# Block 0 of a two-layer kernel: tiles 2 and 3 turned by DMA, V in two halves, eps added on GpSimd, one input tile loaded later

## The chip, the cores and the metric

The kernel runs on one core of a Trainium2 chip. The metric is the device time of one execution in microseconds (us).

PE is TensorE (matmul), PEld its weight load, DVE is VectorE, ACT is ScalarE, POOL is GpSimd, SP is the engine that issues nearly all DMAs.

## The reference, cut to what matters

```python
x = x + A(layernorm(x), wqkv, wo)     # local attention, 32 heads of 32, window 8, dilation 2
x = x + B(layernorm(x), W_gate, W_up, W_down)   # (relu(gate) * up) @ W_down
x = x + A(...); x = x + B(...)        # once more, same weights
# x: 2048 x 1024 bf16
```

The kernel works in four blocks of 512 tokens, each of four tiles of 128 tokens. The layer norm makes `xn` (tokens on partitions); the projections need it turned, `xnT` (features on partitions). V, Q and K of block 0 are the first real work of TensorE.

## The kernel before

The norm of block 0, where the program starts. All four tiles are turned by TensorE (`turn`: eight 128x128 transposes into PSUM, then two copies); tiles 2 and 3 in between the V chunks.

```python
def aggr(t):                                   # DVE: mean, var, then var + eps
    ...
    on("v", nc.vector.tensor_scalar, vpe[t][:], mv[:, 1:2], EPS, None, op0=ALU.add)
    power(t)
def power(t):                                  # POOL: (var + eps) ** -0.5
    on("g", nc.gpsimd.tensor_tensor, rstd[t][:], vpe[t][:], neg_half[:, 0:1], op=ALU.pow)
...
hold["later"] = {2: (lambda: (turn(2), copy(2, "a", 0), copy(2, "v", 1))),
                 4: (lambda: (turn(3), copy(3, "v", 0), copy(3, "a", 1)))}

def v_first(ln):                               # (chunk, first tile, last tile + 1)
    plan = [(c, 0, 2) for c in range(6)] + [(c, 2, 4) for c in range(6)] + [(c, 0, 4) for c in range(6, KC)]
...
QK_FIRST = [(nm, c) for c in range(KC) for nm in ("q", "k")]          # block 0: q0 k0 q1 k1 ...
```

After Q and K of block 0, VectorE makes the q-k products of that block, then its softmax and its sum over V, then the products of block 1: one chain. Every 512-wide result of TensorE goes into one of six PSUM banks and holds it until ScalarE or VectorE has read it.

Of the kernel before, what the change touches and what calls it, by code (L numbers as in the profile page):

```python
# [9 lines left out]
ALU = mybir.AluOpType  # L10
ACT = mybir.ActivationFunctionType
# [3 lines left out]
D = 1024  # L15
# [5 lines left out]
KC = D // P  # L21
BLK = 512
TPB = BLK // P
# [13 lines left out]
def kernel(  # L37
# [130 lines left out]
        xt = xpool.tile([P, D], BF16, name=f"x{t}")  # L168
        x_tiles.append(xt)

    def load_x(b):
        for t in range(b * TPB, (b + 1) * TPB):
            if t == 0:
                sp_dma(x_tiles[t][:, 0:SLAB], x_dram[t * P:(t + 1) * P, 0:SLAB])
                nc.scalar.dma_start(x_tiles[t][:, SLAB:D], x_dram[t * P:(t + 1) * P, SLAB:D])
            elif t == 2:
                nc.scalar.dma_start(x_tiles[t][:], x_dram[t * P:(t + 1) * P, :])
            else:
                sp_dma(x_tiles[t][:], x_dram[t * P:(t + 1) * P, :])

    load_x(0)


    slab = {}
# [5 lines left out]
    def want_v(key, mid, end):  # L190
        for g in range(2):
            want((key, g), wqkv_v[:, :, 2 * D + g * SLAB:2 * D + (g + 1) * SLAB], mid if g == 0 else end)
# [105 lines left out]
    def ln_first():  # L298
        hold = {"xnT": xnT_pool.tile([P, TPB, KC, P], BF16, tag="xnT", name="xnT_first")}
        xna = big_tile([P, TPB, D], "xn_first", True)  # L300
        last = {}

        def on(eng, f, *args, **kwargs):
            if eng == "v":
                dv(f, *args, **kwargs)
            elif eng in last:
                with tc.issue_after(last[eng]):
                    last[eng] = f(*args, **kwargs).ins
            else:
                last[eng] = f(*args, **kwargs).ins  # L310

        def small(name, bufs=4):
            return stat_pool.tile([P, 1], F32, tag="f" + name, name=name, bufs=bufs)

        mean, vpe, rstd, bst = {}, {}, {}, {}

        def bn(t, half):
            if half == 0:
                bst[t] = stat_pool.tile([P, 2, 6], F32, tag="bst", name="bst")
            on("v", nc.vector.bn_stats, bst[t][:, half, :], x_tiles[t][:, half * SLAB:(half + 1) * SLAB])  # L320

        def aggr(t):
            mv = stat_pool.tile([P, 2], F32, tag="mv", name="mv", bufs=4)
            on("v", nc.vector.bn_aggr, mv[:], bst[t][:].rearrange("p a b -> p (a b)"))
            vpe[t], mean[t] = small("vpe1"), mv[:, 0:1]
            on("v", nc.vector.tensor_scalar, vpe[t][:], mv[:, 1:2], EPS, None, op0=ALU.add)
            power(t)

        def power(t):
            rstd[t] = small("rstd1")  # L330
            on("g", nc.gpsimd.tensor_tensor, rstd[t][:], vpe[t][:], neg_half[:, 0:1], op=ALU.pow)

        def act_stats(t):
            st1 = stat_pool.tile([P, 2], F32, tag="st1", name="st1")
            on("a", nc.scalar.activation, xna[:, t, :], x_tiles[t][:], ACT.Identity, accum_out=st1[:, 0:1])
            on("a", nc.scalar.activation, xna[:, t, :], x_tiles[t][:], ACT.Square, accum_out=st1[:, 1:2])
            return st1

        def act_vpe(t, st1):
            mn = small("mean1")  # L340
            on("v", nc.vector.tensor_scalar, mn[:], st1[:, 0:1], 1.0 / D, None, op0=ALU.mult)
            nvar = small("nvar1")
            on("v", nc.vector.scalar_tensor_tensor, nvar[:], st1[:, 0:1], mn[:], st1[:, 1:2], op0=ALU.mult, op1=ALU.subtract)
            vpe[t], mean[t] = small("vpe1"), mn[:]
            on("v", nc.vector.tensor_scalar, vpe[t][:], nvar[:], -1.0 / D, EPS, op0=ALU.mult, op1=ALU.add)
            power(t)

        def apply(t):
            on("v", nc.vector.tensor_scalar, xna[:, t, :], x_tiles[t][:], mean[t], rstd[t][:],
               op0=ALU.subtract, op1=ALU.mult)  # L350

        tps = {}

        def turn(t):
            tps[t] = [psum.tile([P, KC // 2, P], BF16, tag="acc", name=f"tp{h}") for h in range(2)]
            for c in range(KC):
                with pe_group():
                    tail_pe[0] = nc.tensor.transpose(tps[t][c // (KC // 2)][:, c % (KC // 2), :],  # L358
                                                     xna[:, t, c * P:(c + 1) * P], ident[:]).ins

        def copy(t, eng, h):
            f = nc.vector.tensor_copy if eng == "v" else nc.scalar.copy
            on(eng, f, hold["xnT"][:, t, h * (KC // 2):(h + 1) * (KC // 2), :], tps[t][h][:])

        warm = small("warm")
        on("a", nc.scalar.activation, warm[:], ones[:, 0:1], ACT.Identity)
        scratch(14)
        bn(0, 0)
        bn(0, 1)
        aggr(0)  # L370
        bn(1, 0)
        bn(1, 1)
        aggr(1)
        st1 = act_stats(2)
        apply(0)
        turn(0)
        apply(1)
        copy(0, "a", 1)
        copy(0, "a", 0)
        turn(1)  # L380
        act_vpe(2, st1)
        copy(1, "v", 0)
        copy(1, "a", 1)
        bn(3, 0)
        bn(3, 1)
        apply(2)
        aggr(3)
        apply(3)
        hold["later"] = {2: (lambda: (turn(2), copy(2, "a", 0), copy(2, "v", 1))),
                         4: (lambda: (turn(3), copy(3, "v", 0), copy(3, "a", 1)))}  # L390
        return hold


# [20 lines left out]

    def v_first(ln):
        st = att[0]
        plan = [(c, 0, 2) for c in range(6)] + [(c, 2, 4) for c in range(6)] + [(c, 0, 4) for c in range(6, KC)]

        def f_(i, c, t0, t1):
            def f():  # L420
                if i == 0:
                    st["vT"] = big_tile([P, KC, BLK], "vT_0", True)
                acc = psum.tile([P, BLK], F32, tag="acc", name="acc_v")
                cols = slice(t0 * P, t1 * P)
                with pe_group():
                    for kc in range(KC):
                        mm(acc[:, cols], lhsT=slab[("v0", c // 4)][:, kc, (c % 4) * P:(c % 4 + 1) * P],
                           rhs=ln["xnT"][:, t0:t1, kc, :], start=(kc == 0), stop=(kc == KC - 1))
                tail_act[0] = nc.scalar.copy(st["vT"][:, c, cols], acc[:, cols]).ins
                if i in ln["later"]:  # L430
                    ln["later"][i]()
            return f

        at, out = 0.0, []
        for i, (c, t0, t1) in enumerate(plan):
            out.append((at, f_(i, c, t0, t1)))
            at += GRP * (t1 - t0) / TPB
        return out
# [7 lines left out]

    khalo = {}

    QK_FIRST = [(nm, c) for c in range(KC) for nm in ("q", "k")]
    QK_ORDER = [("q", 0), ("q", 1)]  # L450
    for c in range(2, KC):
        QK_ORDER += [("q", c), ("k", c - 2)]
# [3 lines left out]
    def qk_steps(n, ln, key, staged=False):  # L456
# [46 lines left out]
                sp_dma(t[:], (q_d if nm == "q" else k_d)[c, :, b * BLK - lead:(b + 1) * BLK])  # L503
            return f

        order = QK_FIRST if n < NB else QK_ORDER
        steps = [f_(nm, c) for nm, c in order]
        if not staged:
            return steps
# [8 lines left out]
    def head_mm(n):  # L518
        st = att[n]
        st["L"] = psum_l.tile([P, W, P], F32, tag="L", name=f"L_{n}")  # L520
        with pe_group():
            for wh in range(2):
                for tq in range(TPB):
                    mm(st["L"][32 * tq:32 * tq + 32, WH * wh:WH * (wh + 1), :], lhsT=sel[:],
                       rhs=st["s"][:, WH * wh:WH * (wh + 1), tq * P:(tq + 1) * P],
                       start=True, stop=True, skip_group_check=True, tile_position=(0, 32 * tq))
# [287 lines left out]
    def spread(steps, at, gap):  # L814
        for i, f in enumerate(steps):
            ev.append((at + gap * i, f))
# [37 lines left out]
    t_fill = t_wo0 + GRP * KC  # L854
    t_gu0 = t_fill + GRP * (4 * KC - ahead)

    want_v("v0", t_v0 + GRP * 5, t_qk0)
    want_qk("qk01", t_qk1 + GRP * KC, t_v1)
    want_v("v123", t_v3 + GRP * KC / 2, t_qk2)
    want_qk("qk23", t_qk2 + GRP * 2 * KC, t_gu0)  # L860
    want_wo(0, t_fill, t_fill)
    for at, f in v_first(ln_a[0]):
        ev.append((t_v0 + at, f))
    ev.append((0.35, lambda: load_x(1)))
    ev.append((t_v0 + GRP * 5 + 0.6, lambda: load_x(2)))
    ev.append((t_v0 + GRP * 5 + 0.7, zero_v))
    stats, apply, turn, ln_a[1] = ln_steps(1, "a", True, range(TPB))
    for t in range(TPB):
        ev.append((t_v0 + 7.5 + 2.0 * t, stats[t]))
# [2 lines left out]
    ev.append((t_qk0 + 4.0, store_v(0)))  # L872
    ev.append((t_qk0 + 18.0, lambda: load_x(3)))
    spread(qk_steps(0, ln_a[0], "qk01"), t_qk0, GRP)
    spread(prod_sum_steps(0), t_qk0 + 3.5, 4.4)
    spread(load_v_steps(0), t_qk0 + 19.0, 1.0)
    ln1(2, t_qk0 + 10.0, t_qk1 + 10.5, True, 4.5)
    qk1, puts1, gets1 = (part[0::2] + part[1::2] for part in qk_steps(1, ln_a[1], "qk01", True))
# [4 lines left out]
    spread(v_steps(1, ln_a[1], "v123", True), t_v1, GRP)  # L883
    ev.append((t_v2 + 3.0, store_v(1)))
    spread(v_steps(2, ln_a[2], "v123", True), t_v2, GRP)
    ev.append((t_v2 + 3.2 * GRP, lambda: head_mm(0)))
    spread(softmax_steps(0), t_v2 + 3.3 * GRP, 0.01)
    t_pv0 = t_v2 + 2.2 * GRP + 10.0
    spread(pv_steps(0), t_pv0, 4.3)
    for i in range(4):  # L890
        ev.append((t_pv0 + 8.6 * (i + 1), store_o(0, 2 * i, 2 * i + 2)))
# [130 lines left out]
```

## Time and profile before

| | before |
|---|---|
| median of the first six executions | 1619.27 us (1618.89 to 1619.68) |
| PE busy | 1608.1 of 1617.5 us |
| first V matmul | 9.83 us |
| first Q matmul | 24.67 us |
| VectorE continuously at work | about 36 to 230 us |

The busy line of the page (busy us, share of the span, instructions):

```profile
PE 1608.1 (99%) x7505; PEld 784.1 (48%) x7554; DVE 1138.3 (70%) x963; ACT 475.8 (29%) x971; POOL 176.1 (11%) x164
```

The view of the waits of PE, two of its four lines (who waited for whom: us in total, times, longest):

```profile
PE scratch L132 <- DVE ones L290: 1.5, 1, 1.5
PE acc_v L132 <- DMA w_v<-in_A_wqkv_dram: 0.9, 1, 0.9
```

The largest, 1.5 us, is the very start of the program; the 0.9 us are the wait of V for its first weights. All the waits that the view lists for PE, 3.5 us together, end by 9.83 us: the kernel is bound by TensorE from then on. The timeline of PE (start us, length us, engine, line, operation, out<-in, shapes, count, and in brackets what ended an idle stretch):

```profile
9.83 2.79 PE L132 MATMUL acc_v<-xnT_first,w_v 128*128 128x256 bf16 x24 [0.86 <-DMA w_v<-in_A_wqkv_dram]
12.46 0.61 PE L358 MATMUL tp<-ident,xn_first 128*128 128x128 bf16 x8
12.91 1.91 PE L132 MATMUL acc_v<-xnT_first,w_v 128*128 128x256 bf16 x16
14.66 0.61 PE L358 MATMUL tp<-ident,xn_first 128*128 128x128 bf16 x8
15.10 9.73 PE L132 MATMUL acc_v<-xnT_first,w_v 128*128 128x256 bf16 x72
24.67 1.89 PE L132 MATMUL acc_q<-xnT_first,w_qk_q 128*128 128x512 bf16 x8
```

The first V matmul waits for the first V slab (1 MB), which landed at 9.79 us. The transposes of tiles 2 and 3 take 12.46 to 12.91 and 14.66 to 15.10: 0.89 us of TensorE's time. V takes 14.84 us, from 9.83 to 24.67.

Three more lines: VectorE's timeline at the first output projection and at the first gate.

```profile
166.13 2.48 DVE L106 TENSOR_TENSOR x<-acc_wo,x 128x512 bf16<-128x512 f32 x4
...
171.91 0.55 DVE L106 TENSOR_SCALAR xn_b<-x,mv,rstd 128x1024 bf16<-128x1024 bf16 x1 [1.68 <-POOL rstd L286]
...
199.76 1.28 DVE L106 TENSOR_TENSOR hT<-acc_u,r 128x512 bf16<-128x512 f32 x2
```

VectorE reads the first output-projection group at 166.13, though PE finished it at about 162 us: it is late already, and that lateness is borne by the PSUM banks.

### The profile page before, as it was taken

What the parts mean: (1) busy time and instruction counts of PE and PEld (TensorE: products, weight loads), DVE (VectorE), ACT (ScalarE), POOL (GpSimd) and SP (SyncE); (2) the same over time, 40 slices, a digit from 0 to 9 for tenths busy, and PEclk for the clock granted to TensorE, in tenths of its full rate; (3) what the DMA queues carried; (4) which work ended last, traced back from release to release, by engine and by line L of the source; (5) the groups of instructions that cost most, each with busy time, mean ns of one, the idle gap of its engine ahead of it and who ended that gap; (6) DMA issues with size and microseconds to landing.
All of it is one profiled execution on the core that took longest, in us unless ns stands there. A gap on an engine that the chain in (4) does not pass through costs nothing.

```text
span 1617.5 us, 18722 instructions
## 1 busy us (share of the span) xinstructions
PE 1608.1 (99%) x7505; PEld 784.1 (48%) x7554; DVE 1138.3 (70%) x963; ACT 475.8 (29%) x971; POOL 176.1 (11%) x164
## 2 busy tenths in 40 slices
PE   9999999999999999999999999999999999999999
PEld 6646544444444445444454444544445444444444
DVE  6999979996989698929489293893939939311211
ACT  4853311131116313603136031361313311131110
POOL 2300100010003002300053000530005100000000
PEclk9999999999999999999999999999999999999999
DMA  9868867697669767794747948479574884755452
GB/s 295 184 197 251 213 173 244 182 213 206 209 189 216 202 183 216 188 248 144 229 160 202 240 152 230 153 203 254 160 231 155 207 240 156 209 171 167 155 169 66
DMA packets 408440, 317.92 MB, mean 197 GB/s; under 512 B 166432, under 2 KB 389024, under 8 KB 407840
## 3 DMA queue, kind: packets, MB, share of 16 engines
q1 hardware_dynamic: 407776, 316.13, 69.4%
q8 instruction: 59, 0.97, 0.2%
q10 hardware_dynamic: 576, 0.59, 0.1%
q14 instruction: 29, 0.24, 0.1%
HBM read 266.29 MB, written 34.66 MB: 186 GB/s over the span
## 4 chain that ended last, share of the span: by engine, by line
PE 99%; DMA 0%; issue 0%; SPq 0%; DVE 0%; DVEq 0%
PE acc_u L132 24%; PE acc_g L132 24%; PE dacc L132 18%; PE acc_v L132 7%; PE acc_q L132 7%; PE acc_k L132 7%; PE acc_wo L132 7%; PE dacc_pair L132 6%; DMA w_v<-in_A_wqkv_dram 0%; PE tp L358 0%; SPq L121 0%; PE L L132 0%; DVE x L778 0%; SPq L118 0%; DVEq L1017 0%
## 5 line engine op out<-in xcount | busy, mean ns | idle before, releaser
L132 PE MATMUL acc_g<-xnT_b,w_g 128*128 128x512 bf16 x1792 | 423.3, 379 | 0.0
L132 PE MATMUL acc_u<-xnT_b,w_u 128*128 128x512 bf16 x1792 | 423.3, 379 | 0.0
L731 ACT ACTIVATE r<-acc_g 128x512 bf16<-128x512 f32 x224 | 133.6, 596 | 728.7 <-PE acc_g L132 703.8
L106 DVE TENSOR_TENSOR hT<-acc_u,r 128x512 bf16<-128x512 f32 x224 | 151.0, 687 | 243.3 <-PE acc_u L132 240.8
L132 PE MATMUL dacc<-w_d,hT 128*128 128x512 bf16 (+1 forms) x1372 | 300.4, 375 | 1.5
L132 PEld LDWEIGHTS <-hT 128*128 128x128 bf16 x1820 | 178.1, 98 | 209.0
L132 PEld LDWEIGHTS <-w_g 128*128 128x128 bf16 x1792 | 175.4, 98 | 211.4
L132 PEld LDWEIGHTS <-w_u 128*128 128x128 bf16 x1792 | 175.3, 98 | 211.4
L106 DVE TENSOR_TENSOR pv<-a,vhm 128x4096 bf16<-128x4096 bf16 x64 | 143.6, 2285 | 0.0
L778 DVE TENSOR_TENSOR x<-dacc,x 128x512 bf16<-128x512 f32 (+1 forms) x38 | 24.5, 673 | 154.1 <-PE dacc L132 154.1
L549 DVE TENSOR_TENSOR t<-q,k 128x2048 f32<-128x2048 bf16 x56 | 128.0, 2292 | 6.7 <-ACT k L485 4.6
L106 DVE TENSOR_TENSOR t<-q,k 128x2048 f32<-128x2048 bf16 x56 | 127.5, 2287 | 3.9 <-ACT k L485 2.4
L106 DVE TENSOR_TENSOR pv<-pv 128x1024 bf16<-128x1024 bf16 (+1 forms) x128 | 113.8, 952 | 0.0
L132 PE MATMUL acc_wo<-w_o,oT 128*128 128x512 bf16 x498 | 111.1, 379 | 0.7
L249 POOL TENSOR_TENSOR st_b<-st_b,neg_half 128x1 f32<-128x1 f32 x29 | 43.8, 1517 | 609.9 <-ACT st_b L248 609.9
L562 DVE TENSOR_TENSOR ac<-ac,t 128x2048 f32<-128x2048 f32 x48 | 109.7, 2285 | 0.3
L106 DVE TENSOR_TENSOR ac<-ac,t 128x2048 f32<-128x2048 f32 x48 | 109.7, 2285 | 0.0
L490 POOL COPY kh<-k 128x14 bf16<-128x14 bf16 x40 | 53.7, 1348 | 506.5 <-ACT k L485 410.4
L132 PE MATMUL dacc_pair<-w_d,hT 128*128 128x512 bf16 x413 | 95.5, 379 | 0.4
L132 PEld LDWEIGHTS <-oT 128*128 128x128 bf16 x512 | 50.1, 98 | 60.4
L244 ACT ACTIVATE xn_b<-x 128x1024 bf16<-128x1024 bf16 x29 | 30.3, 1047 | 128.6 <-DVE x L106 66.5
L410 ACT CAST vT<-acc_v 128x512 bf16<-128x512 f32 x56 | 32.7, 586 | 54.0 <-PE acc_v L132 54.0
(131 smaller groups left out, 1226.8 us busy)
## 6 DMA issues: line engine op xcount, KB each, us to landing
w_g<-in_B_W_gate_dram SPq DMA_DIRECT2D x56, 1024.0 KB, 7.2
w_u<-in_B_W_up_dram SPq DMA_DIRECT2D x56, 1024.0 KB, 5.5
w_d<-in_B_W_down_dram SPq DMA_DIRECT2D x48, 1024.0 KB, 6.0
w_o<-in_A_wo_dram SPq DMA_DIRECT2D x16, 1024.0 KB, 6.6
vhm<-v_d SPq DMA_DIRECT2D x32, 284.0 KB, 6.7
v_d<-vT SPq DMA_DIRECT2D x8, 1024.0 KB, 9.0
oT<-o_d SPq DMA_DIRECT2D x32, 256.0 KB, 4.5
w_d<-in_B_W_down_dram SPq DMA_DIRECT2D x16, 512.0 KB, 3.7
```

The source lines that it names most:

```text
L106: tail_dve[0] = f(*args, **kwargs).ins
L132: tail_pe[0] = nc.tensor.matmul(*args, **kwargs).ins
L244: nc.scalar.activation(xn, xt[:], ACT.Square, accum_out=sq)
L249: nc.gpsimd.tensor_tensor(rstd, vpe, neg_half[:, 0:1], op=ALU.pow)
L410: tail_act[0] = nc.scalar.copy(st["vT"][:, c, :], acc[:]).ins
L490: nc.gpsimd.tensor_copy(khalo[n][:, c, :], k[:, BLK:BLK + HALO])
L549: nc.vector.tensor_tensor(t[:], i0, i1, op=ALU.mult)
L562: nc.vector.tensor_tensor(o, ac[:], t[:], op=ALU.add)
L731: tail_act[0] = nc.scalar.activation(rs[j][:], acc[:], ACT.Relu).ins
L778: run = dv if n < NB - 2 else (lambda f, *args, **kwargs: f(*args, **kwargs))
```

## The change

Its intent: start V earlier (the fourth input tile no longer stands ahead of the first V slab; the eps addition leaves VectorE), and take the 16 transposes of tiles 2 and 3 off TensorE, by giving them to the DMA queues while TensorE makes all eight V chunks on tiles 0 and 1. Q and K of block 0 are put in another order, and what follows them is moved two groups later.

```diff
-    load_x(0)
+    load_x(0, range(TPB - 1))
...
+    ev.append((0.05, lambda: load_x(0, [TPB - 1])))        # behind the first V slab
+    spread(ln_a[0]["rest"], 0.25, 0.01)                    # norm of tiles 2, 3 and both DMA transposes
...
-            on("v", nc.vector.tensor_scalar, vpe[t][:], mv[:, 1:2], EPS, None, op0=ALU.add)
+            on("g", nc.gpsimd.tensor_scalar, vpe[:], var, sign, EPS, op0=ALU.mult, op1=ALU.add)
...
+        def turn_dma(t):
+            return lambda: sp_dma(hold["xnT"][:, t, :, :], xna[:, t, :], True)
...
-        plan = [(c, 0, 2) for c in range(6)] + [(c, 2, 4) for c in range(6)] + [(c, 0, 4) for c in range(6, KC)]
+        plan = [(c, t, t + 2) for t in (0, 2) for c in range(KC)]
...
-        order = QK_FIRST if n < NB else QK_ORDER
+        order = QK_STAGED if staged else QK_ORDER          # block 0: q0 q1 q2 k0 q3 k1 ...
-    spread(prod_sum_steps(0), t_qk0 + 3.5, 4.4)
+    spread(prod_sum_steps(0), t_qk0 + GRP * K_STEP[0] + 1.8, 4.4)
-    ev.append((t_v2 + 3.2 * GRP, lambda: head_mm(0)))
+    ev.append((t_v2 + 5.2 * GRP, lambda: head_mm(0)))
# cut: softmax and the sum over V of block 0 also two groups later; apply of tile 1 in halves;
# mean and square of tile 2 scaled on ScalarE; the loads of block 1 in two parts
```

The issue order of the DMAs is now: first V slab, fourth input tile, second V slab, first half of the Q weights, the two transposes, second half of the Q weights, K weights with the tiles of block 1 between.

More of the change, by code (lines that the diff above doesn't have):

```diff
@@ L169, with load_x @@
         x_tiles.append(xt)
-    def load_x(b):
-        for t in range(b * TPB, (b + 1) * TPB):
+    def load_x(b, tiles=range(TPB)):
+        for t in (b * TPB + i for i in tiles):
             if t == 0:
@@ L313, in small @@
             return stat_pool.tile([P, 1], F32, tag="f" + name, name=name, bufs=bufs)
-        mean, vpe, rstd, bst = {}, {}, {}, {}
+        mean, rstd, bst = {}, {}, {}
         def bn(t, half):
@@ L324, in aggr, with power @@
             on("v", nc.vector.bn_aggr, mv[:], bst[t][:].rearrange("p a b -> p (a b)"))
-            vpe[t], mean[t] = small("vpe1"), mv[:, 0:1]
-            on("v", nc.vector.tensor_scalar, vpe[t][:], mv[:, 1:2], EPS, None, op0=ALU.add)
-            power(t)
-        def power(t):
-            rstd[t] = small("rstd1")
-            on("g", nc.gpsimd.tensor_tensor, rstd[t][:], vpe[t][:], neg_half[:, 0:1], op=ALU.pow)
+            mean[t] = mv[:, 0:1]
+            power(t, mv[:, 1:2], 1.0)
+        def power(t, var, sign):
+            rstd[t], vpe = small("rstd1"), small("vpe1")
+            on("g", nc.gpsimd.tensor_scalar, vpe[:], var, sign, EPS, op0=ALU.mult, op1=ALU.add)
+            on("g", nc.gpsimd.tensor_tensor, rstd[t][:], vpe[:], neg_half[:, 0:1], op=ALU.pow)
@@ L333, in act_stats @@
         def act_stats(t):
             st1 = stat_pool.tile([P, 2], F32, tag="st1", name="st1")
-            on("a", nc.scalar.activation, xna[:, t, :], x_tiles[t][:], ACT.Identity, accum_out=st1[:, 0:1])
-            on("a", nc.scalar.activation, xna[:, t, :], x_tiles[t][:], ACT.Square, accum_out=st1[:, 1:2])
-            return st1
-        def act_vpe(t, st1):
-            mn = small("mean1")
-            on("v", nc.vector.tensor_scalar, mn[:], st1[:, 0:1], 1.0 / D, None, op0=ALU.mult)
+            on("a", nc.scalar.activation, xna[:, t, :], x_tiles[t][:], ACT.Identity, scale=1.0 / D, accum_out=st1[:, 0:1])
@@ L342, in act_vpe, with act_power @@
+            on("a", nc.scalar.activation, xna[:, t, :], x_tiles[t][:], ACT.Square, scale=float(D) ** -0.5,
+               accum_out=st1[:, 1:2])
+            return st1
+        def act_power(t, st1):
+            mean[t] = st1[:, 0:1]
             nvar = small("nvar1")
-            on("v", nc.vector.scalar_tensor_tensor, nvar[:], st1[:, 0:1], mn[:], st1[:, 1:2], op0=ALU.mult, op1=ALU.subtract)
-            vpe[t], mean[t] = small("vpe1"), mn[:]
-            on("v", nc.vector.tensor_scalar, vpe[t][:], nvar[:], -1.0 / D, EPS, op0=ALU.mult, op1=ALU.add)
@@ L346, in act_vpe, with apply @@
-            power(t)
-        def apply(t):
-            on("v", nc.vector.tensor_scalar, xna[:, t, :], x_tiles[t][:], mean[t], rstd[t][:],
+            on("v", nc.vector.scalar_tensor_tensor, nvar[:], mean[t], mean[t], st1[:, 1:2], op0=ALU.mult, op1=ALU.subtract)
+            power(t, nvar[:], -1.0)
+        def apply(t, half=None):
+            cols = slice(0, D) if half is None else slice(half * SLAB, (half + 1) * SLAB)
+            on("v", nc.vector.tensor_scalar, xna[:, t, cols], x_tiles[t][:, cols], mean[t], rstd[t][:],
@@ L376, in ln_first, with rest @@
         turn(0)
-        apply(1)
+        apply(1, 0)
+        apply(1, 1)
+        copy(0, "a", 0)
         copy(0, "a", 1)
-        copy(0, "a", 0)
         turn(1)
-        act_vpe(2, st1)
         copy(1, "v", 0)
-        copy(1, "a", 1)
-        bn(3, 0)
-        bn(3, 1)
-        apply(2)
-        aggr(3)
-        apply(3)
-        hold["later"] = {2: (lambda: (turn(2), copy(2, "a", 0), copy(2, "v", 1))),
-                         4: (lambda: (turn(3), copy(3, "v", 0), copy(3, "a", 1)))}
+        copy(1, "v", 1)
+        def rest():
+            act_power(2, st1)
+            bn(3, 0)
+            apply(2)
+            bn(3, 1)
+            aggr(3)
+            apply(3)
+        hold["rest"] = [rest, turn_dma(2), turn_dma(3)]
         return hold
@@ L429, in f @@
                 tail_act[0] = nc.scalar.copy(st["vT"][:, c, cols], acc[:, cols]).ins
-                if i in ln["later"]:
-                    ln["later"][i]()
             return f
@@ L447 @@
     khalo = {}
-    QK_FIRST = [(nm, c) for c in range(KC) for nm in ("q", "k")]
+    QK_STAGED = [(nm, c) for c in range(KC) for nm in ("q", "k")]
     QK_ORDER = [("q", 0), ("q", 1)]
@@ L855 @@
     t_gu0 = t_fill + GRP * (4 * KC - ahead)
-    want_v("v0", t_v0 + GRP * 5, t_qk0)
+    want_v("v0", t_v0 + GRP * 6, t_qk0)
     want_qk("qk01", t_qk1 + GRP * KC, t_v1)
@@ L863 @@
         ev.append((t_v0 + at, f))
-    ev.append((0.35, lambda: load_x(1)))
-    ev.append((t_v0 + GRP * 5 + 0.6, lambda: load_x(2)))
-    ev.append((t_v0 + GRP * 5 + 0.7, zero_v))
+    ev.append((0.05, lambda: load_x(0, [TPB - 1])))
+    spread(ln_a[0]["rest"], 0.25, 0.01)
+    ev.append((0.35, lambda: load_x(1, [0, 1])))
+    ev.append((0.45, lambda: load_x(1, [2, 3])))
+    ev.append((t_v0 + GRP * 6 + 0.6, lambda: load_x(2)))
+    ev.append((t_v0 + GRP * 6 + 0.7, zero_v))
     stats, apply, turn, ln_a[1] = ln_steps(1, "a", True, range(TPB))
@@ L885 @@
     spread(v_steps(2, ln_a[2], "v123", True), t_v2, GRP)
-    ev.append((t_v2 + 3.2 * GRP, lambda: head_mm(0)))
-    spread(softmax_steps(0), t_v2 + 3.3 * GRP, 0.01)
-    t_pv0 = t_v2 + 2.2 * GRP + 10.0
+    ev.append((t_v2 + 5.2 * GRP, lambda: head_mm(0)))
+    spread(softmax_steps(0), t_v2 + 5.3 * GRP, 0.01)
+    t_pv0 = t_v2 + 4.2 * GRP + 10.0
     spread(pv_steps(0), t_pv0, 4.3)
```

## The prediction

> **What bounds the kernel.** TensorE. The page's busy table gives PE 1608.1 of 1617.5 us (99%); its listed waits, 3.5 us, all end by 9.83 us; then the chain of waits is PE. So only the start of the first V matmul, PE work and new PE stalls can move the time; none is 2% (32 us).
>
> **Start.** The timeline has the first V matmul at 9.83 us; the first V slab landed at 9.79, the last PSUM copy of tile 1 ended at 9.60. The fourth input tile landed at 6.41, 1.7 us after the one before it; without it I estimate the slab at 9.0. The copies then decide. DVE loses two 0.15 us eps adds, but GpSimd gains one before each power. Tile 1's power took 0.79 us beside tile 0's apply, 0.55 alone; the Trainium skill (GPSIMD Engine Reference, 1. Specifications) says GpSimd shares its SBUF interface with VectorE; the trace agrees. So tile 1's rstd comes 0.2 to 0.4 us later, but its two copies split better. First V matmul: about 9.3 us (-0.5).
>
> **PE work.** Sixteen transposes leave the V stage, 0.056 us each: -0.89. Sixteen 128x512 matmuls (0.216) become 32 halves (0.109): +0.03.
>
> **New wait, tiles 2 and 3.** The first eight half-chunks last 64 x 0.109 = 7.0 us, so PE wants both DMA transposes at about 16.3 us. They are issued behind two V slabs and half the Q weights, which landed at 15.51 us with the same bytes ahead. The skill (DMA: Bandwidth & Descriptors, Queues, rings and completion order) says each DMA engine consumes descriptors in ring order; in the trace landings follow issue order. Block 1's DMA transposes landed 2.3 to 3.2 us after the last load ahead of the pair. So I estimate the second at 17.4 to 18.7, say 18.0: PE waits about 1.7 us, and Q starts at about 25.1 instead of 24.67. The front is then +0.4, not -1.4.
>
> **New wait, much later.** Block 0 now makes Q before K: the first K comes two groups (3.45 us) later relative to PE, so the VectorE chain, continuous to 230 us, runs 3.45 us later. One later gap shrinks by about 1.0 us: at 171.9 us VectorE waited 1.68 us for rstd behind another power on GpSimd, and the changed order swaps these. For each PE group I compared its start with the release of the PSUM bank six groups earlier. The residual margins at about 203, 214 and 231 us are 2.7, 2.5 and 1.2 us. A lag of 2.4 us gives one stall of about 1.2 us at 231 us; without the swap's gain, about 2.2. Afterwards VectorE idles between gates; the rest moves rigidly.
>
> **Sum.** 1619.2 + 0.4 + 1.2 = 1620.8 us. Range 1618.0 to 1622.8. Faster by over 2%: 0.01; within 2%: 0.98; slower: 0.01.
>
> **What shows it.** First V matmul 9.0 to 9.7 us in the timeline; a PE wait on the second DMA transpose at 16 to 18.5 us; first Q matmul at 24.5 to 25.8; first q-k product about 3.5 us later relative to Q; VectorE's add onto the first output-projection group 3.4 us later, without a PE stall; a PE wait on VectorE near 231 us; nothing new after 240 us.
>
> **What would make it wrong.** If the transposes overtake or overlap the loads, the wait vanishes and the time falls to about 1618.5 or, without the second stall too, 1617.6. If a transpose lands later still, or the GpSimd swap brings nothing, it rises to 1622 or more.

## The result, and the profile after

| | before | after |
|---|---|---|
| median of six executions each | 1619.27 us (1618.89 to 1619.68) | 1619.74 us (1618.61 to 1620.80) |
| span of the profiled execution | 1617.5 us | 1618.0 us |
| first V matmul | 9.83 us | 9.56 us |
| first Q matmul | 24.67 us | 24.78 us |

The ratio is 1.0002, 95% interval 0.9989 to 1.0015: the same time. (A ratio here is the mean time of one kernel's fast runs over that of the other's of the same rounds, so not quite the ratio of the medians.) The page and the waits of PE after:

```profile
PE 1610.2 (100%) x7554; PEld 784.5 (48%) x7554; DVE 1137.4 (70%) x958; ACT 474.2 (29%) x970; POOL 179.7 (11%) x168
```

```profile
PE acc_v L132 <- DMA xnT_first<-xn_first: 0.9, 1, 0.9
PE acc_v L132 <- DMA w_v<-in_A_wqkv_dram: 0.8, 1, 0.8
```

The larger busy time of PE is no more work: the trace of the kernel before lacks 49 of 7554 matmul records. The new wait is for `xnT_first`, a DMA transpose. PE's timeline after:

```profile
9.56 7.36 PE L132 MATMUL acc_v<-xnT_first,w_v 128*128 128x256 bf16 x64 [0.77 <-DMA w_v<-in_A_wqkv_dram]
17.80 7.15 PE L132 MATMUL acc_v<-xnT_first,w_v 128*128 128x256 bf16 x64 [0.88 <-DMA xnT_first<-xn_first]
24.78 5.34 PE L132 MATMUL acc_q<-xnT_first,w_qk_q 128*128 128x512 bf16 x24
```

The transposes are gone from PE, and the first half of V is 64 matmuls in one piece, but 7.36 us long where 64 x 0.109 us is 7.0: inside it PE waited 0.19 us at 13.25 for the second V slab, which landed at 13.20. Measured between the starts of matmuls (the listed 0.88 counts from a modelled end), the wait for the transpose is 1.04 us. So V is now 15.22 us long, and the sum closes:

| term | us |
|---|---|
| V before (9.83 to 24.67) | 14.84 |
| 16 transposes gone | -0.89 |
| 16 matmuls of 512 become 32 of 256 | +0.03 |
| wait for the second V slab | +0.19 |
| wait for the DMA transpose of tile 3 | +1.04 |
| sum; measured 9.56 to 24.78 | 15.21; 15.22 |

The start is 0.27 us earlier, the stage 0.38 us longer: Q starts 0.11 us later. From there on the two traces run in parallel, 0.11 us apart, to the last matmul (1613.82 and 1613.92). The remaining 0.37 us between the two spans arise after it, where the kernels are the same: from the start of the last matmul to the end it is 3.69 us before, 4.07 after and 3.89 in a repeat of the changed kernel, and 3.34 to 4.18 in all 14 traces, so this stretch alone scatters by 0.84 us. In between there is no scatter: from the first matmul of block 1 (at 51.5 to 57.3 us) to the last matmul every trace takes 1561.52 us, but for that of experiment 7, which takes 1562.72. What the other kernels differ in is therefore read before that matmul.

When and how long the transposes were under way, from the view of the tile `xnT_first` (duration of the issue in ns, min/median/max, first and last start; then time from issue to landing):

```profile
L121 SPq DMA_TRANSPOSE xnT_first<-xn_first x2: 1343/1631/1919, 11.4 to 13.7; - x2
DMA to landing us min/median/max: 3.9/4.7/5.4
```

The second was issued at 13.74, when tile 3 had been normed, and landed 3.92 us later, at 17.66. TensorE had wanted it at 16.76.

The DMA queues meanwhile, from the view by windows (the last two numbers of a line: share of the DMA engines' time, GB/s):

```profile
12.00:13.00 1.00, 1.00 (x12) 0.85 (x9) 0.21 (x1) 0.37 (x1) 0.61 (x2) 1.00 1.04 377
...
14.00:15.00 1.00, 1.00 (x11) 0.90 (x10) 0.00 (x0) 0.37 (x1) 0.00 (x0) 1.00 0.95 94
15.00:16.00 1.00, 1.00 (x12) 0.89 (x10) 0.00 (x0) 0.37 (x1) 0.00 (x0) 1.00 0.51 115
16.00:17.00 1.00, 0.92 (x9) 0.57 (x6) 0.00 (x0) 0.42 (x2) 0.00 (x0) 1.00 1.28 287
```

From 12 to 13 us, with the V slabs and the Q weights under way, the queues move 377 GB/s; from 14 to 17 us, when the transposes are most of what is left in them, 94 to 287. The packets that the trace keeps of each DMA (the views print only their sums) show a standstill. The transposes move in packets of 256 bytes, which no other load here uses at that time. Twenty of these packets, begun between 13.85 and 14.44 us, all end only between 15.71 and 15.76, just after the load of Q weights ahead is through (its last completion write is at 15.38). The repeat and the traces of experiments 6, 7 and 12 show the same, 18 to 23 packets each. So the transposes had begun early and then stood until the load ahead of them was through; why they do is not shown. And VectorE later:

```profile
169.68 2.48 DVE L106 TENSOR_TENSOR x<-acc_wo,x 128x512 bf16<-128x512 f32 x4
...
174.52 0.55 DVE L106 TENSOR_SCALAR xn_b<-x,mv,rstd 128x1024 bf16<-128x1024 bf16 x1 [0.73 <-POOL rstd L286]
...
202.37 1.28 DVE L106 TENSOR_TENSOR hT<-acc_u,r 128x512 bf16<-128x512 f32 x2
```

Against PE (0.11 us later), VectorE is 3.44 us later at the output projection and 2.50 us at the first gate: the wait of 1.68 us for GpSimd has shrunk to 0.73. Both are as predicted. VectorE's lateness reaches the place of the feared stall too (its products there start at 231.50 us, 228.89 before), but the groups of PE follow each other there without a wait, and no wait of PE is listed after 20 us:

```profile
229.18 1.89 PE L132 MATMUL acc_g<-xnT_b,w_g 128*128 128x512 bf16 x8
230.90 1.89 PE L132 MATMUL acc_u<-xnT_b,w_u 128*128 128x512 bf16 x8
```

### The profile page after: what moved, and what is told of

Same layout as the page of the kernel before. It is cut to its first block, busy times and chain, and to the rows that moved or that the text cites. A ratio compares the mean times of both kernels' runs of the same rounds, so it can differ in the third digit from the quotient of the medians.

```text
span 1618.0 us, 18775 instructions
## 1 busy us (share of the span) xinstructions
PE 1610.2 (100%) x7554; PEld 784.5 (48%) x7554; DVE 1137.4 (70%) x958; ACT 474.2 (29%) x970; POOL 179.7 (11%) x168
## 4 chain that ended last, share of the span: by engine, by line
PE 99%; DMA 1%; DVE 0%; issue 0%; SPq 0%; POOL 0%; DVEq 0%
PE acc_u L132 24%; PE acc_g L132 24%; PE dacc L132 18%; PE acc_k L132 7%; PE acc_q L132 7%; PE acc_wo L132 7%; PE acc_v L132 6%; PE dacc_pair L132 6%; DMA x<-in_A_x_dram 0%; DMA xnT_first<-xn_first 0%; DVE xn_first L106 0%; SPq L121 0%; DVE bst L106 0%; POOL rstd L308 0%; PE L L132 0%
```

## The experiments

Two theories of the missing gain. A: the transposes by DMA arrive late, and TensorE gives back in waiting what it saved in work. B: the later VectorE chain costs something. For A there are sub-theories: A1, the transposes come late because of what stands ahead of them in the queues; A2, they are slow in themselves and hold up what is behind. Where a median is compared with "the changed kernel", its median was 1619.74 (six executions) and 1619.39 (five, in experiment 1). Every set had its own runs of the kernel before: 1619.26 beside experiments 1 to 4, 1619.44 beside 5 to 8, 1619.30 beside 9 to 12. These sets ran on three different chips, so medians of different sets are best compared through their own kernel before.

### 1. The changed kernel again

No edit.

> The changed kernel again, for its spread. Its first six executions ran from 1618.6 to 1620.8 us, those of the kernel before from 1618.9 to 1619.7. Theory A (the wait for the DMA transpose of tile 3 takes back what the front gained): the landing of that transpose moves from one execution to the next, so this profile shows a wait before the second half of V that differs from the 1.06 us of the first profile by about as much as the whole time differs, and the executions spread by 1.5 to 2.5 us again. Theory B (the later VectorE chain costs something in some executions): the wait before the second half of V is the same, and PE waits on VectorE near 170 us, where the bank was free only 0.10 us before it was wanted.

Measured: median 1619.39 us (1619.00 to 1620.10), ratio 1.0001 (0.9989 to 1.0014). The wait for the transpose was 1.05 us, for the second slab 0.20, first Q at 24.64. The wait is the same within 0.01 us, and in three further traces with this front it was 1.02, 1.05 and 0.74 (experiments 6, 7 and 12). So theory A, as I had put it, finds no support: the two profiled executions of this kernel differ by 0.3 us and their waits do not. PE waited nowhere near 170 us either, so nothing here speaks for B. The spread was smaller this time, 1.1 us. No execution at the slow end (1620.8) was profiled, so the spread stays open; up to 0.84 us of such a spread can arise after the last matmul, as said above.

### 2. Tiles 2 and 3 turned by TensorE

```diff
-        hold["rest"] = [rest, turn_dma(2), turn_dma(3)]
+        hold["rest"] = [rest]
+        hold["later"] = {3: (lambda: (turn(2), copy(2, "a", 0), copy(2, "v", 1))),
+                         5: (lambda: (turn(3), copy(3, "v", 0), copy(3, "a", 1)))}
```

> The changed kernel with tiles 2 and 3 turned by TensorE as before, between V half-chunks, all else kept. Theory A: the wait of 1.06 us for the DMA transpose goes, 16 transposes of 0.056 us (0.89 us) come back, so the first Q matmul is at 24.5 to 24.7 instead of 24.78 us, the time is 0.1 to 0.3 us under the changed kernel, and the executions spread by under 0.9 us, as those of the kernel before. Theory B: the spread stays at 2 us, as the order of Q and K is the changed one.

Measured: median 1618.57 us (1618.46 to 1619.30), ratio 0.9997 (0.9983 to 1.0011). PE's timeline:

```profile
9.30 3.65 PE L132 MATMUL acc_v<-xnT_first,w_v 128*128 128x256 bf16 x32 [0.29 <-DVE xnT_first L106]
12.79 0.61 PE L357 MATMUL tp<-ident,xn_first 128*128 128x128 bf16 x8
...
24.17 5.34 PE L132 MATMUL acc_q<-xnT_first,w_qk_q 128*128 128x512 bf16 x24
```

No wait remains after 9.30, the transposes are back (12.79 to 13.24, 14.99 to 15.43), and Q starts at 24.17, 0.61 us before the changed kernel: 0.26 from the start, 0.19 and 1.04 from the two waits, less 0.89 for the transposes, make 0.60. V is 14.87 us long, as before the change. This undoes one part of the change and shows theory A for the V stage: there the DMA turn cost 0.35 us more than it saved. Whether the earlier start (the first slab landed at 8.94 us, not 9.51) belongs to it too is not settled, and of the 0.8 us between the medians of experiments 1 and 2 only 0.5 lie before the last matmul in the traces, the rest after it. The second half of the K weights landed at 26.94 us instead of 30.36.

### 3. The transposes ahead of the Q weights

```diff
-    spread(ln_a[0]["rest"], 0.25, 0.01)
+    spread(ln_a[0]["rest"], 0.15, 0.01)
```

> The changed kernel with both DMA transposes issued ahead of the first half of the Q weights, not behind it. Theory A (they wait in the rings behind 1 MB of weights): the second lands at 15.0 to 16.2 us instead of 17.66, PE does not wait for it, Q starts at 23.6 to 23.9 us. Then the second half of the K weights, which landed at 30.36, is wanted at about 29.7, so 0.7 us of the 1.06 may come back as a wait for it: the time falls by 0.3 to 1.0 us. Rival A2 (the transposes are slow in themselves, whatever is ahead of them): the second lands at 17 us or later again, Q starts within 0.3 us of 24.78, and the time is unchanged.

Measured: median 1620.42 us (1619.87 to 1622.58), ratio 1.0011 (0.9998 to 1.0023). The median rose by about 1 us instead of falling; the interval just includes 1.

```profile
16.44 7.16 PE L132 MATMUL acc_v<-xnT_first,w_v 128*128 128x256 bf16 x64 [0.17 <-DMA xnT_first<-xn_first]
...
31.66 1.08 PE L132 MATMUL acc_k<-xnT_first,w_qk_k 128*128 128x512 bf16 x4 [2.02 <-DMA w_qk_k<-in_A_wqkv_dram]
```

The second transpose, issued at 13.29 with only the first one ahead of it (the second V slab had landed at 12.06, the first transpose landed at 14.09), landed at 16.39: 3.1 us. The wait before the second half of V fell from 1.04 to 0.33 us, so A1 has its share, and Q started at 23.43. No packet stood still here. The 3.1 us are 1.23 for the issue on SP, about 1.4 for the 1024 packets (14.46 to 15.91) and 0.5 until the landing is seen. What a plain copy would have taken on this front was not run, so this experiment does not judge A2. And SP, which issues in order, could not issue the Q weights before tile 3 was normed: the K weights landed at 31.61, and PE waited 2.18 us (start to start) for them. The wait moved from V to K and grew. The two slowest of the five executions, 1621.68 and 1622.58 us, have a mean granted clock of 0.999, the other three 1.000. Experiment 6 shows a wait for K that halves the clock for a while, so the same may have happened in these two. No trace of them was kept, and the figure is rounded (it is 0.999 in an execution of 1619.10 us in experiment 1 too), so this is not shown.

### 4. The same, with the K weights pulled ahead

```diff
+    spread(ln_a[0]["rest"], 0.15, 0.01)
-    ev.append((0.45, lambda: load_x(1, [2, 3])))
+    ev.append((0.45, lambda: load_x(1, [2])))
+    ev.append((t_v0 + GRP * 6 + 0.35, lambda: load_x(1, [3])))
# and the norm of that tile on VectorE after the first two q-k products
```

> The third kernel with, besides, the eighth input tile loaded behind the second half of the K weights and its norm placed on VectorE after the first two q-k products. If theory A holds, the K weights land at about 29.7 us, PE has no wait after the first V slab other than 0.2 us for the second, Q starts at 23.6 to 23.9, and the time is 0.9 to 1.2 us under the changed kernel, about 1618.6, below the kernel before too. If the moved norm delays the VectorE chain, PE waits on VectorE near 169 us (margin 0.10 us) by that delay, and part of it is lost.

Measured: median 1619.81 us (1619.34 to 1621.92), ratio 1.0006 (0.9994 to 1.0019): a miss. Here the second transpose, issued at 13.26 just as in experiment 3, landed at 18.08, 4.8 us later, and PE waited 2.06 us for it; the K weights (30.78) then came in time. Up to there the two programs are the same, with the Q weights following closely behind in both. So the time from issue to landing varied by 1.7 us between two executions of the same code, but not the moving of the data: the packets of this transpose were through by 16.08 (15.91 in experiment 3). One packet of 16 KB, an instruction fetch, then ran from 16.07 to 17.03, and the last two of the transpose's 32 completion writes came only at 17.02 and 17.03. In experiment 3 such a fetch began at 16.27, after all 32 writes. So about 1.1 of the 1.7 us looks like a chance meeting with that fetch (that both used the same DMA engine is inferred from the times); the rest stays open.

### 5. Plain copies in the transposes' place (wrong results on purpose)

```diff
-            return lambda: sp_dma(hold["xnT"][:, t, :, :], xna[:, t, :], True)
+            return lambda: sp_dma(hold["xnT"][:, t, :, :].rearrange("p k n -> p (k n)"), xna[:, t, :])
```

> The changed kernel with its two DMA transposes replaced by plain DMA copies of the same 256 KB at the same place (wrong results on purpose). Theory A1 (only the place behind 1 MB of Q weights counts): the second copy lands within 0.4 us of 17.6 and the wait before the second half of V stays near 1 us. Theory A2 (a transpose is itself slow in the rings, and holds up what is behind it): the second copy lands at 16.3 to 16.9, the wait falls to 0 to 0.4 us, the second half of the Q weights lands at 19.0 to 20.0 us instead of 21.35, the second half of the K weights at 28.0 to 29.0 instead of 30.3, and the time falls by 0.6 to 1.1 us with a spread under 1 us.

Measured: median 1618.92 us (1618.19 to 1620.24), ratio 0.9996 (0.9983 to 1.0008); the result is wrong, as meant. The second copy was issued at 13.89 and landed at 17.30, 3.4 us later; PE waited 0.56 us instead of 1.04. The second half of the Q weights landed at 20.67 (21.35 with transposes), of the K weights at 29.79 (30.36). Both sub-theories missed their numbers: by this pair of traces about half of the wait belongs to the transposing (0.48 of 1.04 us), the other half would have been there for any DMA in this place. The wait alone is weak evidence, as it was 0.74 us in experiment 12 with transposes. Counted from the landing of the load ahead (first half of the Q weights), it is clearer: the second transpose landed 1.79 to 1.83 us after it in all five traces with this front, the second plain copy 1.32 us after it (17.30 against 15.98). And most of the delay of the later weights is no matter of transposing: the K weights came 2.85 us later than in experiment 2 with plain copies, 3.42 with transposes. The issue times of SP show one cause. With transposes (changed kernel):

```profile
3.34 3.74 SPq L121 DMA_DIRECT2D w_qk_q<-in_A_wqkv_dram  x1
11.40 4.26 SPq L121 DMA_TRANSPOSE xnT_first<-xn_first  x2
15.71 0.57 SPq L121 DMA_DIRECT2D w_qk_q<-in_A_wqkv_dram  x1
```

without any (experiment 2):

```profile
3.39 4.54 SPq L121 DMA_DIRECT2D w_qk_q<-in_A_wqkv_dram  x2
7.97 2.16 SPq L121 DMA_DIRECT2D x<-in_A_x_dram  x2
```

In the changed kernel SP issues nothing between 7.1 and 11.4 us and only the two transposes until 15.7, because it waits for the norm of tiles 2 and 3 and because these two issues themselves hold it for 1.34 and 1.92 us; the second half of the Q weights goes out at 15.71, in experiment 2 it had gone out by 7.9. By then the queues hold little but the two transposes, and those stand still (115 GB/s in the window from 15 to 16 us above, against 389 in experiment 2).

### 6. The old order of Q and K, with the DMA transposes

```diff
-        order = QK_STAGED if staged else QK_ORDER
+        order = QK_STAGED if n < NB else QK_ORDER
# and the old places of the products, softmax and sum over V of block 0
```

> The changed kernel with the old order of Q and K chunks in block 0 and the old places of its q-k products and softmax; the DMA transposes stay. Theory: K is then wanted two groups earlier, its second half at about 27.3 us, and it still lands at about 30.3, so PE waits about 3.0 us there and the time is 2.8 to 3.2 us over the changed kernel; the margin of the PSUM bank at the seventh output-projection group goes from 0.10 back to 3.5 us. Rival: the weights come in time in either order and the time is unchanged.

Measured: median 1624.09 us (1623.18 to 1624.25, four executions), ratio 1.0025 (1.0011 to 1.0039). Slower by 4.4 us than the changed kernel, more than the 2.8 to 3.2 expected.

```profile
30.56 1.24 PE L132 MATMUL acc_k<-xnT_first,w_qk_k 128*128 128x512 bf16 x4 [2.98 <-DMA w_qk_k<-in_A_wqkv_dram]
31.60 3.46 PE L132 MATMUL acc_q<-xnT_first,w_qk_q 128*128 128x512 bf16 x8
```

The wait for K is there as expected (3.14 us from start to start). But the next group of eight takes 3.46 us, where every other takes 1.89. The window after it (in the last part of the line: granted clock, DMA share, GB/s):

```profile
31.36:34.77 3.41, 3.41 (x10) 1.39 (x9) 2.88 (x3) 0.59 (x1) 2.79 (x4) 0.50 1.20 111
```

TensorE ran at half clock for 3.41 us right after its idle stretch: about 1.7 us more. This is the missing part: 0.21 us of wait for the first half of the K weights (landed at 26.45), 3.14 for the second, about 1.7 of half clock, less 0.22 for an earlier start of Q, make 4.8; the first matmul of block 1 is 4.94 us later. The page "TensorE: Matmul & The Clock Gate" of the Trainium skill (Part 1: The HAM clock gate) tells of half clock as the state of an idle TensorE and of a window of about 3.4 us; the trace agrees with the length. Experiment 12 tests the cause.

### 7. One more VectorE operation in the chain

```diff
-            dv(nc.vector.tensor_tensor, a[:], d[:], _ap(rs, 0, [[0, W], [1, P]]), op=ALU.mult)
+            for _ in range(2 if n == 0 else 1):
+                dv(nc.vector.tensor_tensor, a[:], d[:], _ap(rs, 0, [[0, W], [1, P]]), op=ALU.mult)
```

> The changed kernel with one softmax product of block 0 done twice on VectorE, 1.23 us more in a chain that has no slack until 230 us. Theory from the true PSUM banks of the built program: the least margin is 0.10 us, at the seventh output-projection group (170.4 us), so PE waits 1.13 us there and nowhere later (next margins 1.2 us and more shrink by nothing more), and the time rises by 1.1 us. By the recorded prediction's rule (the bank of six groups earlier) there would also be a wait near 231 us of about 1 us or more. Rival (there is hidden room): no wait, no change.

Measured: median 1620.02 us (1619.56 to 1621.11), ratio 1.0003 (0.9990 to 1.0015); the mean, 1620.30, is 0.8 us over the mean (1619.54) of the eleven executions of the changed kernel. But the median is 0.58 us over that of the kernel before of its own set, where the changed kernel was 0.47 and 0.13 over, so the times alone do not show the 1.1 us that was expected; the trace does. It has one long wait more:

```profile
171.73 3.61 PE L132 MATMUL acc_wo<-w_o,oT 128*128 128x512 bf16 x16 [1.04 <-DVE x L106]
```

From start to start it is 1.21 us, where 1.13 was expected, and there is none near 231 us; from block 1 to the last matmul this trace takes 1.20 us more than every other. (A wait of 0.22 us for the K weights, landed at 30.77, comes from the front.) The margin of each PE group, worked out from the banks that the built program assigns and the times of the trace (changed kernel, three of the smallest and the one that the prediction feared):

```
group               bank  starts   bank's last user   released   margin
7th acc_wo             1  170.47   1st acc_wo           170.37     0.10
acc_k                  1  180.83   7th acc_wo           179.69     1.14
acc_g                  4  205.00   1st acc_u            203.06     1.95
acc_u (feared)         1  230.90   acc_g at 222.27      224.79     6.11
```

The banks are not handed out in a fixed turn of six: the group at 230.90 uses a bank that ScalarE had freed 6.11 us before, not the one six groups earlier. The least margin is 0.10 us at the seventh output-projection group. So the changed order of Q and K used up the slack of the VectorE chain almost to the end, but not beyond, and costs no time. The same calculation for experiment 6, with the old order, gives 3.55 us there.

### 8. TensorE turns, and the old order of Q and K

The edits of experiments 2 and 6 together.

> The second experiment's kernel (tiles 2 and 3 turned by TensorE) with the old order of Q and K in block 0 too. Theory: without DMA transposes the second half of the K weights lands at 26.9 us and is wanted at 26.8, so PE waits 0 to 0.4 us; the time is within 0.4 us of the second experiment's 1618.6, the spread is under 1 us, and the margin at the seventh output-projection group is 3.5 us again. So the new order of Q and K is needed only because of the DMA transposes.

Measured: median 1618.75 us (1618.67 to 1619.34), ratio 0.9995 (0.9981 to 1.0009); first V at 9.24, K weights at 26.56, no wait for them, margin at the seventh output-projection group 3.56 us. With TensorE turning, the old order of Q and K costs nothing, and the VectorE chain has its slack again: the new order is needed only because of the DMA turn.

### 9. Experiment 2 again

> The second experiment's kernel again, since it was the fastest (1618.57 us): if the gain is real, the median is 1618.4 to 1618.8 us again, 0.5 to 0.9 us under the kernel before, with first Q matmul near 24.2 us; if that was one chip's luck, the two medians are within 0.3 us of each other.

Measured: median 1618.40 us (1618.25 to 1619.38), ratio 0.9995 (0.9983 to 1.0008); first V at 9.04, first Q at 23.90, V 14.86 us long. Of the ten executions of this kernel, eight lie below the lowest of the 18 of the kernel before that ran beside them (1618.85). Both medians are 0.7 to 0.9 us lower. The intervals of the ratios contain 1, so this is a steady small gain in the medians, not a verdict. Up to the last matmul the two traces gain 0.51 and 0.77 us, and this comes from the start alone: V is as long as before the change (14.86 and 14.87 against 14.84). A further 0.18 and 0.21 us lie after the last matmul, where nothing was changed.

### 10. eps back on VectorE

```diff
-            on("g", nc.gpsimd.tensor_scalar, vpe[:], var, sign, EPS, op0=ALU.mult, op1=ALU.add)
+            on("v", nc.vector.tensor_scalar, vpe[:], var, sign, EPS, op0=ALU.mult, op1=ALU.add)
```

(on the kernel of experiment 2)

> The second experiment's kernel with the eps additions back on VectorE. By the recorded prediction eps on GpSimd makes tile 1's rstd 0.2 to 0.4 us later, so here tile 1's power would end 0.2 to 0.4 us earlier and the first V matmul come earlier by about that. By the trace of the second experiment (the statistics' end to the end of the power: 1.10 us there, 1.06 us in the kernel before) the two ways cost the same: first V matmul within 0.15 us of 9.30, time within 0.2 us of that kernel's.

Measured: median 1618.87 us (1618.57 to 1619.70), ratio 0.9998 (0.9986 to 1.0011); first V at 9.49, because the slab landed at 9.44. So the start cannot judge; the chain of the statistics can. Changed kernel (eps on GpSimd), tile 0's statistics, then tile 1's:

```profile
4.87 0.21 DVE L106 BATCH_NORM_AGGREGATE mv<-bst 128x2 f32<-128x12 f32 x1
6.26 0.21 DVE L106 BATCH_NORM_AGGREGATE mv<-bst 128x2 f32<-128x12 f32 x1
...
6.56 0.37 POOL L308 TENSOR_SCALAR vpe<-mv 128x1 f32<-128x1 f32 x1 [0.51 <-DVE mv L106]
7.01 0.56 POOL L308 TENSOR_TENSOR rstd<-vpe,neg_half 128x1 f32<-128x1 f32 x1
```

Experiment 10 (eps on VectorE):

```profile
4.86 0.21 DVE L106 BATCH_NORM_AGGREGATE mv<-bst 128x2 f32<-128x12 f32 x1
6.48 0.21 DVE L106 BATCH_NORM_AGGREGATE mv<-bst 128x2 f32<-128x12 f32 x1
...
6.96 0.79 POOL L308 TENSOR_TENSOR rstd<-vpe,neg_half 128x1 f32<-128x1 f32 x1 [0.98 <-DVE vpe L106]
```

From the end of tile 0's aggregate to the end of tile 1's power it is 2.49 us with eps on GpSimd (5.08 to 7.57), 2.68 with eps on VectorE (5.07 to 7.75). In all three traces with eps on VectorE it is 2.68, in ten of the eleven with eps on GpSimd 2.49 (2.59 in experiment 5). GpSimd does lose time to VectorE (its addition takes 0.37 us beside VectorE's apply; the one for tile 0, beside VectorE's statistics, took 0.19, as did the one for tile 3 with VectorE idle), but VectorE reaches tile 1's aggregate 0.22 us earlier. The prediction's 0.2 to 0.4 us later had the wrong sign. My "within 0.15 us of 9.30" for the first V matmul missed as well, at 0.19, through the slab.

### 11. The kernel before, with only the fourth tile loaded later

```diff
-    load_x(0)
+    load_x(0, range(TPB - 1))
+    ev.append((0.05, lambda: load_x(0, [TPB - 1])))
```

(and the norm of tiles 2 and 3 emitted after that load)

> The kernel before with only its fourth input tile loaded behind the first V slab. The slab lands at 8.9 to 9.5 us instead of 9.79; tile 1's last copy, at 9.60 us before, then decides, so the first V matmul comes at 9.5 to 9.7 instead of 9.83 and the time falls by 0.1 to 0.3 us. If nothing but the slab decided it would be 9.0 to 9.5.

Measured: median 1619.44 us (1618.83 to 1619.92), ratio 0.9999 (0.9986 to 1.0013): inconclusive. In the profiled execution the very first tile landed at 4.20 us instead of 3.67, the slab at 10.01, and the first V matmul came at 10.06, outside the 9.5 to 9.7 that I expected. From the first tile's landing to the first V matmul it is 5.86 us, 6.16 before, which would be a gain of 0.3, but one trace with a late start doesn't settle it.

### 12. The wait of experiment 6 filled with work

```diff
+                if n == 0 and nm == "k" and c == 0:
+                    scratch(14)        # 14 matmuls of 128x512, results unused
                 acc = psum.tile([P, BLK], F32, tag="acc", name=f"acc_{nm}")
```

> The sixth experiment's kernel with 14 idle-filling 128x512 matmuls (about 3.0 us, results unused) ahead of the first K chunk, in the place of its wait of 3.1 us for the K weights. There, the granted clock fell to half for 3.41 us just after that wait, and the time rose by 1.7 us beyond the wait. Theory (the idle stretch made the clock fall): with TensorE kept busy the granted clock stays 1.0, the K matmuls after the wait start 0.216 us apart and not 0.43, and the time falls by 1.5 to 1.9 us to about 1622.4. Rival (the clock fell for another reason, or the extra matmuls push K later): no fall, or a rise.

Measured: median 1622.47 us (1621.85 to 1622.91, four executions), ratio 1.0019 (1.0005 to 1.0032): 1.6 us under experiment 6. In the traces it is 30.85 us from the first Q matmul to block 1, where experiment 6 took 32.78.

```profile
26.14 3.18 PE L132 MATMUL scratch<-ones 128*128 128x512 bf16 x14
29.16 2.10 PE L132 MATMUL acc_k<-xnT_first,w_qk_k 128*128 128x512 bf16 x8
31.10 1.89 PE L132 MATMUL acc_q<-xnT_first,w_qk_q 128*128 128x512 bf16 x8
```

```profile
31.36:34.77 3.41, 3.41 (x18) 2.25 (x17) 2.75 (x2) 1.13 (x3) 2.51 (x4) 1.00 1.80 121
```

The clock stayed at 1.00, the group after the wait took 1.89 us, and the K weights (30.13) were waited for as before, only busily but for a last 0.15 us. The idle stretch was what cost the 1.7 us.

## Why the prediction was right or wrong

The measured 1619.74 us lies in the range and in the class with the 0.98. That says little: the range, 1618.0 to 1622.8, holds the median of every kernel here but experiment 6, and 1.2 of the 1.6 us that were forecast as a rise came from a stall that did not exist. Point by point:

- **Bound by TensorE, so nothing near 2%.** Right.
- **Start, 9.3 us predicted, 9.0 to 9.7.** Measured 9.56 and 9.40. But the step was wrong inside: I let the copies decide and estimated the slab at 9.0; the copies ended at 9.26 and the slab, at 9.51 and 9.35, decided. In ten other traces with this load order at the front the slab landed between 8.05 and 9.64. The eps step had the wrong sign (experiment 10).
- **PE work, -0.86 us.** Right: the sum above closes with it.
- **Wait for the second transpose, 1.7 us, landing at 17.4 to 18.7.** The mechanism was right, the term was too large: landing at 17.66 and a wait of 1.04 us. The second transpose landed 1.8 us after the load ahead of it, where I had taken 2.3 to 3.2 from block 1, and PE wanted it at 16.76, not 16.3. I missed 0.19 us of wait for the second V slab. The reason given was partly wrong: I held only the place in the queue, behind two V slabs and half the Q weights, responsible. With no load ahead a transpose still took 3.1 and 4.8 us from issue to landing (experiments 3 and 4), and plain copies in the same place kept about half of the wait (experiment 5).
- **The front worth +0.4 us.** Measured +0.11 in the traces.
- **VectorE 3.45 us later, 1.0 us of it regained by the swap on GpSimd.** Right: 3.44, then 2.50 at the first gate.
- **A stall of 1.2 us at 231 us.** Wrong; none came. The step that failed is "the release of the PSUM bank six groups earlier": the allocator does not hand the banks out in turn. With the program's own bank numbers the margin there is 6.11 us, and the tight place is the seventh output-projection group, 0.10 us, which experiment 7 turned into a stall of 1.21 us.
- **The sum, 1620.8.** Too high by 1.1 us, which is about the stall that did not exist. That the two agree so well is partly luck: the front was 0.3 us better than predicted, and the profiled execution lost 0.37 us after the last matmul.

Where the gain of 1.1 us (0.27 of the start, 0.86 of PE work) went is shown: 1.23 us into two waits for DMA. Experiment 2, without the DMA turn, keeps the gain of the start and is the fastest kernel here, 1618.57 and 1618.40 us. What stays open: why the changed kernel spreads over 2.2 us, how much of its start the later fourth tile brings (experiment 11), and why transposes stand still until the load ahead is through.

## What to carry to other kernels

Moving 0.89 us of work from a full engine to a DMA pays only if the DMA's data lands before it is wanted: here it landed 3.92 us after its issue and was wanted after 3.02. It also ties up the issuing engine, and all loads behind it in that engine's order are late: here the K weights by 3.4 us, which forced a reorder that used up the slack of another engine down to 0.10 us. Read the margin of a buffer from the buffers that the built program really assigns, not from their count. And keep a waiting TensorE busy through a wait as long as that of experiment 6: 3.1 us of it cost 1.7 us more in clock.

## What the Trainium skill lacked or had wrong

- "DMA: Bandwidth & Descriptors", "Latency and other measured facts", gives 261 GB/s for a DMA transpose with a non-contiguous middle dimension and 350 to 400 for a contiguous one. It has no time from issue to landing for a single small one. Here 256 KB from SBUF to SBUF took 3.1 us from issue to landing with only another transpose ahead, of which the packets took about 1.4 us (about 180 GB/s), 3.9 behind 1 MB, and 4.8 in an execution where its last completion writes came after an instruction fetch; the issue alone held SP for 1.2 to 1.9 us. Nor does the page tell of transposes that stand still behind a load (up to 1.9 us for a packet here).
- The same page, "Queues, rings and completion order", says that each DMA engine consumes its descriptors in ring order. That was too little for when a load lands: the first V slab landed at 9.11 to 9.64 us in traces of the changed front with the Q weights issued behind it, at 8.48 and 8.05 where SP issued them after 14 us (experiments 3 and 4), with the same loads ahead. But experiments 2, 8 and 9, with Q weights behind, had 8.94, 8.87 and 8.71, so the cause is not settled.
- "TensorE: Matmul & The Clock Gate", "Part 1: The HAM clock gate", says that the clock falls after at least one idle window of about 3.4 us. Here a wait of 2.98 us (3.14 from start to start) was enough; the half clock began 0.8 us after TensorE had resumed and lasted 3.41 us. Waits of 2.02 and 1.9 us in the profiled executions of experiments 3 and 4 left the matmuls at full speed. In the trace of experiment 6 the clock rose at 7.46 us, fell at 31.36 (seven steps of 3.41 us later) and rose again one step later; in the step that ended at 31.36 TensorE was idle for 2.61 of 3.41 us, in no step of experiment 3 for more than 1.3 around its wait.
- "GPSIMD Engine Reference", "1. Specifications", says that GpSimd shares its SBUF interface with VectorE. The runs agree and give a size: a 128x1 addition took 0.37 us beside a 128x1024 apply and 0.19 with VectorE idle or at its statistics. Even so the addition belonged there (2.49 against 2.68 us for the chain).
- None of the pages tells how a pool hands out PSUM banks; here the assumption of a fixed turn of six led to fear of a stall of 1.2 us where the margin was 6.11 us.
